# Batch 1's attention moved earlier inside the head of a fused linear-attention and MLP kernel

## Chip, cores, metric

The kernel runs on one core of a Trainium2 chip. The metric is device time of one execution in microseconds (us), median of several runs. Executions of one kernel agree within about 0.3%. All profiles are of core 0. A profile's span is 1.8 to 1.9 us shorter than the timed value, so times are compared with times and spans with spans.

## The reference, cut to what matters

```python
# 8 batches, 8 heads, 576 rows, head size 64
kv  = einsum('bhsd,bhse->bhde', k, v)            # K^T V of each head
out = einsum('bhsd,bhde->bhse', q, kv)           # "scores" below
rms = sqrt(mean(out * out, axis=-1) + 1e-6)
x   = (out / rms * g_norm)                       # -> 4608 tokens x 512
h   = x @ w_in                                   # product one, 512 -> 2048
g   = where(h > 0, h, exp(min(h, 0)) - 1)        # elu
y   = g @ w_out                                  # product two, 2048 -> 512
```

## The kernel before

TensorE works through nine groups of 512 tokens: batches 0 to 7 (512 of the 576 rows of each) and a ninth group of the remaining rows. While it computes one batch's two products, the next batch's attention is slipped in between. The work lies in the head of the kernel, where batch 0's product two runs and batch 1's attention is made for the first time.

The kernel fills eight banks of PSUM, TensorE's output memory (a bank is here the room of 512 fp32 values in each partition): one tile `at` of two banks, two tiles of two banks in the pool `ps_m1`, two tiles of one bank in `ps_m2`. A tile is the unit in which the program reserves this memory. Batch 0's output has four token tiles j of 128 tokens. Tiles 2 and 3 are the two halves of one `ps_m1` tile; tiles 0 and 1 have a `ps_m2` tile each.

```python
def mm2(T, j, f0, f1, hold=False):
    if f0 == 0 and (T, j) not in o_ps:
        o_ps[T, j] = ps_m2.tile([P, DM], FP32, name="o_ps", tag="mm2")
    for f in range(f0, f1):
        nc.tensor.matmul(o_ps[T, j], lhsT=gT[T][:, f, j * P : j * P + P],
                         rhs=w_out_sb[:, f, :], start=(f == 0), stop=(f == FC - 1))
    if f1 == FC and not hold:
        mm2_out(T, j)                   # ScalarE copies o_ps to o_sb; a store after odd j

# x_t(h): turn one half of the scaled rows (xs) and copy it out with g_norm
def turn(ps=None):
    if h == 0:
        st["xt"] = at_tile(BF16).rearrange("p (h c t) -> p h c t", h=2, c=KC)
    xt = st["xt"][:, h]                 # x0 and x1: two halves of the same PSUM tile ...
    if ps is not None:
        xt = ps.bitcast(BF16)...        # ... unless another one is given
    # 8 transposes into xt; then x0 is copied by ScalarE, x1 by VectorE

# ---- loads (cut) ----
edges = (0, 512, 1024, 1536, 2048)      # w_in in four pieces
...
for name in "kv": fetch_packed_kv(name, 1, slice(0, 2))   # first halves of K and V
load_w_out(8, 10)
for name in "kv": fetch_packed_kv(name, 1, slice(2, 4))   # second halves

# ---- batch 0's product two with batch 1's attention inside (cut) ----
both = ps_m1.tile([P, 2, G], FP32, name="o_ps", tag="mm1")
for a in range(2):
    o_ps[0, 2 + a] = both[:, a, :]
order = (2, 3, 0, 1)
for j in order: mm2_quarter(0, j, 0)
at["q"]()                               # q transposes
for j in order: mm2_quarter(0, j, 1)
mm2(0, order[0], 8, 10)
at["kv"]()                              # K^T V
for j in order[1:]: mm2(0, j, 8, 10)
at["se"]({0: None, 1: ps_m1.tile(...)}) # scores; then squares, sums, inverse roots, xs
...
for j in order: mm2(0, j, 10, 12)
for j in order:
    mm2(0, j, 12, FC, hold=j in (2, 3))
    if j == 3:
        mm2_out(0, 2)
        mm2_out(0, 3)
    if j == 0:
        at["x0"]()
...
# ---- batch 1's product one: first two tiles in column halves (cut) ----
for cs in (slice(0, 256), slice(256, G)):
    for f in range(4):
        ...                             # 4 matmuls, 128x256
        if cs.start == 0 and f == 1:
            head_x1()                   # x1 of batch 1
...
# ---- one batch later (cut) ----
at["x0"]()
mm2_quarter(1, 2, 0)
at["x1"](ps_m1.tile([P, 2, G], FP32, name="xt_ps", tag="mm1")[:, 0, :])
mm2_quarter(1, 2, 1)
```

`hold` delays the copies of output tiles 2 and 3 until tile 3 is done.

Of the kernel before, what the change touches and what calls it, by code (L numbers as in the profile page):

```python
# [8 lines left out]
FP32 = mybir.dt.float32  # L9
BF16 = mybir.dt.bfloat16  # L10
# [6 lines left out]
def kernel(  # L17
# [13 lines left out]
    nc = tc.nc  # L31
    P = 128
# [6 lines left out]
    G = J * P  # L39
    RK = S // 64  # L40
    KC = DM // P
    FC = DF // P
# [7 lines left out]
    mlpg = ctx.enter_context(tc.tile_pool(name="mlpg", bufs=2))  # L50
# [13 lines left out]
    w_in_sb = const.tile([P, KC, DF], BF16, name="w_in_sb")  # L64
# [49 lines left out]
    def fetch_packed_kv(name, b, hs=slice(0, 4)):  # L114
        in_ = (k if name == "k" else v)[b].rearrange("h r d -> (h r d)").rearrange(
            "(h p x) -> p h x", h=4, p=P
        )
        nc.gpsimd.dma_start(  # L118
            out=raw[name, b].rearrange("p h j d -> p h (j d)")[:, hs], in_=in_[:, hs]
        )  # L120
# [19 lines left out]
    def load_w_out(f0, f1):  # L140
        fs = slice(f0, f1)
        nc.gpsimd.dma_start(
            out=w_out_sb[:, fs, :], in_=moe_w_out.rearrange("(c p) f -> p c f", p=P)[:, fs, :]
        )
# [17 lines left out]
    xT = {}  # L162

    def at_tile(dtype):
        full = ps_at.tile([P, 1024], FP32, name="at", tag="at")
        return full if dtype == FP32 else full.bitcast(BF16)
# [210 lines left out]
    gT = {}  # L377

    def mm1(T, i, cols=(slice(0, 512),), relu=False, home="m1", between=()):

        if i == 0:
            gT[T] = mlpg.tile([P, FC, G], BF16, name="gT", tag="gT")
        x = xT[T]
        if home == "m2":
            h_ps = [ps_m2.tile([P, G], FP32, name="h_ps", tag="mm2") for _ in range(2)]
            parts = [(a, a + 1, h_ps[a].rearrange("p (a t) -> p a t", a=1)) for a in range(2)]
        else:
            if home == "at":
                both = at_tile(FP32).rearrange("p (a t) -> p a t", a=2)
            else:  # L390
                both = ps_m1.tile([P, 2, G], FP32, name="h_ps", tag="mm1")
            h_ps = [both[:, a, :] for a in range(2)]
            parts = [(0, 2, both)]
        for cs in cols:
            for a in range(2):
                f = 2 * i + a
                for c in range(KC):
                    nc.tensor.matmul(  # L398
                        h_ps[a][:, cs],
                        lhsT=w_in_sb[:, c, f * P : f * P + P],  # L400
                        rhs=x(c, cs),
                        start=(c == 0),
                        stop=(c == KC - 1),
                    )
        return elu(T, i, parts, relu, between)

    def elu(T, i, parts, relu, between=()):
        e = mlpt.tile([P, 2, G], BF16, name="elu_e", tag="elu_e")
        for lo, hi, ps in parts:
            nc.scalar.activation(e[:, lo:hi, :], ps, AF.Exp)  # L410
        for piece in between:
            piece()
        if relu:
            h = mlpt.tile([P, 2, G], BF16, name="elu_h", tag="elu_h", bufs=2)
            for lo, hi, ps in parts:
                nc.scalar.activation(h[:, lo:hi, :], ps, AF.Relu)  # L416
            parts = [(0, 2, h)]

        def rest():
            for lo, hi, h in parts:  # L420
                nc.vector.tensor_scalar(  # L421
                    out=e[:, lo:hi, :],
                    in0=e[:, lo:hi, :],
                    scalar1=1.0,
                    scalar2=1.0,
                    op0=ALU.min,
                    op1=ALU.subtract,
                )
                nc.vector.tensor_tensor(  # L429
                    out=gT[T][:, 2 * i + lo : 2 * i + hi, :],  # L430
                    in0=e[:, lo:hi, :],
                    in1=h,
                    op=ALU.add if relu else ALU.max,
                )

        return rest
# [3 lines left out]
# [5 lines that stand above are left out]
            nc.tensor.matmul(  # L445
                o_ps[T, j],
                lhsT=gT[T][:, f, j * P : j * P + P],
                rhs=w_out_sb[:, f, :],
                start=(f == 0),
                stop=(f == FC - 1),  # L450
            )
        if f1 == FC and not hold:
            mm2_out(T, j)

    def mm2_out(T, j):
        if j % 2 == 0:
            o_sb[T] = outp.tile([P, 2, DM], FP32, name="o_sb", tag="o")
        nc.scalar.copy(o_sb[T][:, j % 2, :], o_ps.pop((T, j)))  # L458
        if j % 2 == 1:
            store(T, j // 2)  # L460

    def mm2_quarter(T, j, i):
        mm2(T, j, 4 * i, 4 * i + 4)

    def store(T, half):
        if T < B:
            nc.sync.dma_start(
                out=out[T * S : T * S + G, :].rearrange("(p j) f -> p j f", j=J)[
                    :, 2 * half : 2 * half + 2, :
                ],  # L470
                in_=o_sb[T],
            )
        else:
            rows = out.rearrange("(i l s) f -> l s i f", l=2, s=S)
            for l in range(2):
                nc.sync.dma_start(
                    out=rows[l, G:S, 2 * half : 2 * half + 2, :],
                    in_=o_sb[T][l * 64 : l * 64 + 64, :, :],
                )
# [7 lines left out]
    for c in range(4):  # L487
# [1 line left out]
        if c == 2:  # L489
            make_identity(nc, ident)  # L490
        fetch_packed_kv("v", 0, slice(c, c + 1))
    edges = (0, 512, 1024, 1536, 2048)
    for lo, hi in zip(edges, edges[1:]):
        load_w_in(slice(lo, hi))
    load_w_out(0, 4)
# [2 lines left out]
    packed_kv(1)  # L498
    for name in "kv":
        fetch_packed_kv(name, 1, slice(0, 2))  # L500
    load_w_out(8, 10)
    for name in "kv":
        fetch_packed_kv(name, 1, slice(2, 4))

    zeros = const.tile([P, 512], BF16, name="zeros")
    nc.vector.memset(zeros, 0.0)  # L506
# [55 lines left out]
    x0 = attp.tile([P, KC, G], BF16, name="xT", tag="xT")  # L562
# [41 lines left out]
    def first(fs, cs):  # L604
# [33 lines left out]
        lhsT=g_row.rearrange("p l d -> p (l d)"),  # L638
        rhs=one,
        start=True,  # L640
        stop=True,
# [48 lines left out]
    ps_m1 = ctx.enter_context(tc.tile_pool(name="ps_m1", bufs=2, space=bass.MemoryType.PSUM, reuse_waits="tile"))  # L690
    ps_m2 = ctx.enter_context(tc.tile_pool(name="ps_m2", bufs=2, space=bass.MemoryType.PSUM, reuse_waits="tile"))

    at, ahead = attention(1), attention(2)
# [14 lines left out]
    order = (2, 3, 0, 1)  # L708
    for j in order:
        mm2_quarter(0, j, 0)  # L710
    at["q"]()
    for j in order:
        mm2_quarter(0, j, 1)
    mm2(0, order[0], 8, 10)
    at["kv"]()
    for j in order[1:]:
        mm2(0, j, 8, 10)
    at["se"]({0: None, 1: ps_m1.tile([P, 2, G], FP32, name="se_ps", tag="mm1")})
    for n in range(2):
        at[f"sq{n}"]()  # L720
# [2 lines left out]
        at[f"inv{n}"]()  # L723
    at["mul0"]()
    at["mul1"]()
    for j in order:
        mm2(0, j, 10, 12)
    unpack_q(2, Q)
    ahead["qd"]()
    for j in order:  # L730
        mm2(0, j, 12, FC, hold=j in (2, 3))
        if j == 3:
            mm2_out(0, 2)
            mm2_out(0, 3)
        if j == 0:
            at["x0"]()

    def fetch(b):
        if b < B:
# [51 lines left out]

    ahead["landed"]()
    fetch(3)
    head_x1 = at["x1"]
    at, ahead = ahead, attention(3)
    ahead["qd"]()
    gT[1] = mlpg.tile([P, FC, G], BF16, name="gT", tag="gT")
    firsts = [ps_m1.tile([P, 2, G], FP32, name="h_ps", tag="mm1") for _ in range(2)]
    for cs in (slice(0, 256), slice(256, G)):
        for f in range(4):  # L800
            for c in range(KC):
                nc.tensor.matmul(  # L802
                    firsts[f // 2][:, f % 2, cs],
                    lhsT=w_in_sb[:, c, f * P : f * P + P],
                    rhs=xT[1](c, cs),
                    start=(c == 0),
                    stop=(c == KC - 1),
                )
            if cs.start == 0 and f == 1:
                head_x1()  # L810
    for i in range(8):
        if i < 2:
            elu(1, i, [(0, 2, firsts[i])], i == 0)()
        else:
            mm1(1, i, relu=i == 4, home="m2" if i in (2, 5) else "m1")()
        if i == 3:
            at["kv"]()
    mm2(1, 0, 0, 8)
# [16 lines left out]
    for T in range(2, NT):  # L835
        at = ahead if T + 1 < NT else None
# [17 lines left out]
    for j, cols in pieces:  # L854
        n = cols.stop - cols.start
        ps = ps_m2.tile([P, DM], FP32, name="o_ps", tag="mm2")[:, 0:n]
        for f in range(FC):
            nc.tensor.matmul(  # L858
                ps,
                lhsT=gT[B][:, f, j * P : j * P + P],  # L860
                rhs=w_out_sb[:, f, cols],
                start=(f == 0),
                stop=(f == FC - 1),
# [35 lines left out]
```

## Time and profile before

| | before |
|---|---|
| time, median of 6 runs | 285.50 us |
| TensorE busy | 97% of the span, full clock |
| start of product two of batch 0 | 29.07 us |
| start of batch 2's K^T V, after four tiles of batch 1's product one | 54.37 us |

Lines of the page of the kernel before: the span, the busy times of the engines with their instruction counts, the granted clock in 40 slices, and the shares of the chain that ended last.

```profile
span 283.7 us, 5180 instructions
...
PE 274.4 (97%) x2131; PEld 130.5 (46%) x2162; DVE 159.9 (56%) x231; ACT 153.1 (54%) x220; POOL 53.5 (19%) x94
...
PEclk9999999999999999999999999999999999999999
...
PE 90%; ACT 3%; DVE 3%; DMA 2%; issue 1%; SPq 0%
```

TensorE bounds the kernel; only its idle moments can be won. They are found in the timeline of TensorE alone, kernel before. The columns are start, duration, engine, line, operation, out<-in, tile and count; what is in brackets is the idle time before the group and what ended it. PE is TensorE, ACT ScalarE, DVE VectorE. Lines L445 and L398 are the matmuls of products two and one, L802 the column-half block. `at<-v_pk,k_pk` is K^T V, `<-kv_sb,qT` the scores, `<-ident,xs` the x transposes.

```profile
29.07 3.62 PE L445 MATMUL o_ps<-w_out_sb,gT 128*128 128x512 bf16 x15
...
39.73 0.41 PE L201 MATMUL at<-kv_sb,qT 64*128 64x64 bf16 x16
...
40.30 4.49 PE L445 MATMUL o_ps<-w_out_sb,gT 128*128 128x512 bf16 x19
44.83 0.62 PE L305 MATMUL at<-ident,xs 128*128 128x128 bf16 x8
45.29 1.03 PE L445 MATMUL o_ps<-w_out_sb,gT 128*128 128x512 bf16 x4
46.69 1.03 PE L802 MATMUL h_ps<-xT,w_in_sb 128*128 128x256 bf16 x8 [0.37 <-ACT xT L312]
47.55 0.61 PE L305 MATMUL at<-ident,xs 128*128 128x128 bf16 x8
48.00 2.99 PE L802 MATMUL h_ps<-xT,w_in_sb 128*128 128x256 bf16 x24
51.04 3.40 PE L398 MATMUL h_ps<-xT,w_in_sb 128*128 128x512 bf16 x15
54.37 0.78 PE L174 MATMUL at<-v_pk,k_pk 64*64 64x64 bf16 x72
...
70.89 0.61 PE L305 MATMUL xt_ps<-ident,xs 128*128 128x128 bf16 x8
71.34 1.03 PE L445 MATMUL o_ps<-w_out_sb,gT 128*128 128x512 bf16 x4
72.35 1.90 PE L398 MATMUL h_ps<-xT,w_in_sb 128*128 128x512 bf16 x7
```

Full-width matmuls (128x512) start every 215.8 ns, the mean of the 948 starts without a break in this trace. A printed idle time is not all that is lost: the end of a matmul is modelled and lies about 0.16 us after the moment at which the next could have started. So the rule is to take the last start, add 0.216, and compare with the next start. The four matmuls at 45.29 should have been followed at 46.15; product one came at 46.69, so 0.53 us were lost, and the wait is for ScalarE's copy of x0 (`ACT xT`). Another 0.2 us were lost ahead of 44.83 (waiting for xs) and, in the single records inside the group at 48.00, 0.2 ahead of the second column half (waiting for x1).

Waits of TensorE from 29 to 52 us, kernel before (total us, times, longest); only the longest entry is shown:

```profile
PE h_ps L802 <- ACT xT L312: 0.4, 1, 0.4
```

ScalarE in the same place, kernel before:

```profile
44.08 1.54 ACT L458 COPY o_sb<-o_ps 128x512 f32<-128x512 f32 x3
45.49 1.14 ACT L312 ACTIVATE xT<-at,g_col 128x1024 bf16<-128x1024 bf16 x1
```

The three output copies (tiles 2, 3 and 0) run back to back after the last inverse root; x0's copy follows.

### The profile page before, as it was taken

How to read it: one execution, taken by the hardware profiler on the slowest of the kernel's cores; microseconds unless marked ns; L12 is line 12 of the kernel's file. 1: busy time of each engine (PE TensorE's matmuls, PEld its weight loads, DVE VectorE, ACT ScalarE, POOL GpSimd, SP SyncE). 2: the span in 40 equal slices, each digit the busy share in tenths (PEclk: the TensorE clock that was granted, in tenths of full speed). 3: DMA queues.
4: the chain of work that ended last, by engine and by line, in shares of the span. 5: the costliest groups of instructions: out<-in, count | busy, mean ns of one | idle time of the engine just before them, and what ended most of it. 6: DMA issues, size and time to landing. Idle time of an engine off the chain costs nothing.

```text
span 283.7 us, 5180 instructions
## 1 busy us (share of the span) xinstructions
PE 274.4 (97%) x2131; PEld 130.5 (46%) x2162; DVE 159.9 (56%) x231; ACT 153.1 (54%) x220; POOL 53.5 (19%) x94
## 2 busy tenths in 40 slices
PE   6999999999999999999999999999999999999994
PEld 2444555545544444445444444444444444444443
DVE  2359315698478636934695468544864486444400
ACT  2779535766496338634773378246923692333311
POOL 7823402251421060104210421012000000000000
PEclk9999999999999999999999999999999999999999
DMA  7999999796993598356944794355253123010122
GB/s 194 204 207 202 207 201 178 225 143 113 196 190 68 150 134 181 76 148 90 208 95 127 105 213 94 98 130 148 49 93 83 77 48 100 2 74 0 74 75 75
DMA packets 55979, 35.99 MB, mean 127 GB/s; under 512 B 32788, under 2 KB 53524, under 8 KB 55956
## 3 DMA queue, kind: packets, MB, share of 16 engines
q0 software_dynamic: 20208, 17.30, 39.7%
q1 hardware_dynamic: 35348, 17.83, 23.6%
q10 hardware_dynamic: 400, 0.52, 0.5%
q8 instruction: 17, 0.28, 0.4%
q14 instruction: 6, 0.05, 0.0%
HBM read 36.70 MB, written 9.44 MB: 163 GB/s over the span
## 4 chain that ended last, share of the span: by engine, by line
PE 90%; ACT 3%; DVE 3%; DMA 2%; issue 1%; SPq 0%
PE h_ps L398 39%; PE o_ps L445 36%; PE o_ps L858 5%; DMA st_q<-in_q_dram 2%; PE at L174 2%; PE h_ps L802 1%; DVE ss L218 1%; PE at L201 1%; PE bank L607 1%; ACT sq L213 1%; PE at L398 1%; PE bank L577 1%; PE bank L529 1%; ACT o_sb L458 1%; PE se_ps L201 1%
## 5 line engine op out<-in xcount | busy, mean ns | idle before, releaser
L398 PE MATMUL h_ps<-xT,w_in_sb 128*128 128x512 bf16 x524 | 123.6, 380 | 0.2
L445 PE MATMUL o_ps<-w_out_sb,gT 128*128 128x512 bf16 x488 | 117.9, 379 | 1.4 <-issue 0.3
L410 ACT ACTIVATE elu_e<-h_ps 128x1024 bf16<-128x1024 f32 (+1 forms) x72 | 70.8, 991 | 83.8 <-PE h_ps L398 79.2
L398 PEld LDWEIGHTS <-w_in_sb 128*128 128x128 bf16 x536 | 50.8, 98 | 61.5 <-DVE xT L333 1.7
L445 PEld LDWEIGHTS <-gT 128*128 128x128 bf16 x512 | 49.6, 98 | 59.1
L421 DVE TENSOR_SCALAR elu_e<-elu_e 128x1024 bf16<-128x1024 bf16 (+1 forms) x75 | 32.3, 431 | 70.5 <-ACT elu_e L410 70.5
L429 DVE TENSOR_TENSOR gT<-elu_e,h_ps 128x1024 bf16<-128x1024 bf16 (+1 forms) x53 | 62.6, 1181 | 5.9 <-DVE elu_e L421 0.5
L218 DVE TENSOR_REDUCE ss<-sq 128x16 f32<-128x1024 bf16 x16 | 19.3, 1218 | 13.4 <-ACT sq L213 12.7
L458 ACT COPY o_sb<-o_ps 128x512 f32<-128x512 f32 x32 | 18.5, 585 | 14.4 <-PE o_ps L445 14.4
L150 POOL COPY q_bf<-q_pk 128x512 bf16<-128x512 bf16 x24 | 14.6, 636 | 23.5 <-DMA q_pk<-in_q_dram 23.5
L416 ACT ACTIVATE elu_h<-h_ps 128x1024 bf16<-128x1024 f32 (+1 forms) x19 | 18.3, 968 | 0.0
L429 DVE TENSOR_TENSOR gT<-elu_e,elu_h 128x1024 bf16<-128x1024 bf16 x19 | 13.2, 693 | 2.9 <-ACT elu_h L416 1.7
L858 PE MATMUL o_ps<-w_out_sb,gT 128*128 128x512 bf16 (+1 forms) x79 | 14.0, 336 | 0.1
L125 POOL COPY gate<-qT 1x1 bf16<-1x1 bf16 x6 | 1.1, 179 | 59.9 <-DMA qT<-q_bf 59.9
L229 DVE TENSOR_TENSOR xs<-at,ss 128x512 bf16<-128x512 f32 x18 | 11.5, 682 | 1.2 <-ACT ss L225 1.2
L104 POOL DMA_DIRECT2D q_pk<-in_q_dram x14 | 10.5, 759 | 4.7 <-issue 1.9
L213 ACT ACTIVATE sq<-at 128x1024 bf16<-128x1024 f32 x9 | 9.4, 1044 | 2.4 <-PE at L201 2.4
L858 PEld LDWEIGHTS <-gT 128*128 128x128 bf16 x80 | 7.7, 98 | 6.4 <-DVE gT L429 0.4
L118 POOL DMA_DIRECT2D v_pk<-in_v_dram x12 | 8.4, 702 | 5.0 <-DMA w_in_sb<-in_moe_w_in_dram 2.9
L118 POOL DMA_DIRECT2D k_pk<-in_k_dram x12 | 8.3, 694 | 5.1 <-DMA w_in_sb<-in_moe_w_in_dram 3.4
L866 ACT COPY o_last<-o_ps 128x512 f32<-128x512 f32 (+1 forms) x5 | 2.5, 500 | 10.8 <-PE o_ps L858 10.8
L529 PE MATMUL bank<-zeros 128*128 128x512 bf16 x19 | 6.6, 465 | 1.4 <-DVE zeros L506 1.2
(73 smaller groups left out, 138.6 us busy)
## 6 DMA issues: line engine op xcount, KB each, us to landing
out_dram<-o_sb SPq DMA_DIRECT2D x16, 512.0 KB, 3.0
q_pk<-in_q_dram POOLq DMA_DIRECT2D x14, 256.0 KB, 5.0
k_pk<-in_k_dram POOLq DMA_DIRECT2D x6, 576.0 KB, 8.1
v_pk<-in_v_dram POOLq DMA_DIRECT2D x6, 576.0 KB, 12.2
w_in_sb<-in_moe_w_in_dram POOLq DMA_DIRECT2D x4, 512.0 KB, 10.9
w_out_sb<-in_moe_w_out_dram POOLq DMA_DIRECT2D x3, 512.0 KB, 15.5
st_q<-in_q_dram SPq DMA_DIRECT2D x2, 512.0 KB, 4.7
st_q<-in_q_dram SPq DMA_DIRECT2D x16, 64.0 KB, 2.5
```

The source lines that it names most:

```text
L118: nc.gpsimd.dma_start(out=raw[name, b].rearrange("p h j d -> p h (j d)")[:, hs], in_=in_[:, hs])
L150: eng.tensor_copy(out=out_, in_=in_)
L213: nc.scalar.activation(sq, se_ps, AF.Square)
L218: nc.vector.reduce_sum(out=ss, in_=sq.rearrange("p c (h e) -> p (c h) e", h=H), axis=AX.X)
L398: nc.tensor.matmul(h_ps[a][:, cs], lhsT=w_in_sb[:, c, f * P : f * P + P], rhs=x(c, cs), start=(c == 0), stop=(c == KC - 1),)
L410: nc.scalar.activation(e[:, lo:hi, :], ps, AF.Exp)
L416: nc.scalar.activation(h[:, lo:hi, :], ps, AF.Relu)
L421: nc.vector.tensor_scalar(out=e[:, lo:hi, :], in0=e[:, lo:hi, :], scalar1=1.0, scalar2=1.0, op0=ALU.min, op1=ALU.subtract,)
L429: nc.vector.tensor_tensor(out=gT[T][:, 2 * i + lo : 2 * i + hi, :], in0=e[:, lo:hi, :], in1=h, op=ALU.add if relu else ALU.max,)
L445: nc.tensor.matmul(o_ps[T, j], lhsT=gT[T][:, f, j * P : j * P + P], rhs=w_out_sb[:, f, :], start=(f == 0), stop=(f == FC - 1),)
L458: nc.scalar.copy(o_sb[T][:, j % 2, :], o_ps.pop((T, j)))
L858: nc.tensor.matmul(ps, lhsT=gT[B][:, f, j * P : j * P + P], rhs=w_out_sb[:, f, cols], start=(f == 0), stop=(f == FC - 1),)
```

## The change

Its intent: let batch 1's scores start earlier, so that the chain behind them is done in time and x0 and x1 can both be turned and copied inside product two; then product one can start full width without a wait. For that, K and V must land earlier, so w_out rows 8 to 10 go behind them.

```diff
-    edges = (0, 512, 1024, 1536, 2048)
+    edges = (0, 512, 768, 1280, 1664, 2048)
...
     for name in "kv":
         fetch_packed_kv(name, 1, slice(0, 2))
-    load_w_out(8, 10)
     for name in "kv":
         fetch_packed_kv(name, 1, slice(2, 4))
+    load_w_out(8, 10)
...
     for j in order:
         mm2_quarter(0, j, 0)
-    at["q"]()
-    for j in order:
+        if j == order[2]:
+            at["q"]()
+    for n, j in enumerate(order):
         mm2_quarter(0, j, 1)
-    mm2(0, order[0], 8, 10)
-    at["kv"]()
-    for j in order[1:]:
-        mm2(0, j, 8, 10)
+        if n in (1, 2):
+            at[f"kv{n - 1}"]()
     at["se"](...)
...
-    for j in order:
-        mm2(0, j, 10, 12)
+    for f in (8, 10):
+        for j in order:
+            mm2(0, j, f, f + 2)
...
     for j in order:
-        mm2(0, j, 12, FC, hold=j in (2, 3))
-        if j == 3:
-            mm2_out(0, 2)
-            mm2_out(0, 3)
-        if j == 0:
-            at["x0"]()
+        mm2(0, j, 12, FC)
+        if j in (3, 0):
+            at["x0" if j == 3 else "x1"]()
...                                    # the column-half block of batch 1 is removed:
     for i in range(8):
-        if i < 2:
-            elu(1, i, [(0, 2, firsts[i])], i == 0)()
-        else:
-            mm1(1, i, relu=i == 4, home="m2" if i in (2, 5) else "m1")()
+        mm1(1, i, relu=i in (0, 4), home="m2" if i in (2, 5) else "m1")()
```

More of the change, by code (lines that the diff above doesn't have):

```diff
@@ L793 @@
     fetch(3)
-    head_x1 = at["x1"]
     at, ahead = ahead, attention(3)
     ahead["qd"]()
-    gT[1] = mlpg.tile([P, FC, G], BF16, name="gT", tag="gT")
-    firsts = [ps_m1.tile([P, 2, G], FP32, name="h_ps", tag="mm1") for _ in range(2)]
-    for cs in (slice(0, 256), slice(256, G)):
-        for f in range(4):
-            for c in range(KC):
-                nc.tensor.matmul(
-                    firsts[f // 2][:, f % 2, cs],
-                    lhsT=w_in_sb[:, c, f * P : f * P + P],
-                    rhs=xT[1](c, cs),
-                    start=(c == 0),
-                    stop=(c == KC - 1),
-                )
-            if cs.start == 0 and f == 1:
-                head_x1()
     for i in range(8):
-        if i < 2:
-            elu(1, i, [(0, 2, firsts[i])], i == 0)()
-        else:
-            mm1(1, i, relu=i == 4, home="m2" if i in (2, 5) else "m1")()
+        mm1(1, i, relu=i in (0, 4), home="m2" if i in (2, 5) else "m1")()
         if i == 3:
```

## The prediction

> **What bounds the kernel.** TensorE. The page gives PE 274.4 us busy of a 283.7 us span (97%), the granted clock is full throughout, and the chain of waits is 90% PE. VectorE (56%), ScalarE (54%) and DMA have slack except at a few joints. Full-width matmuls (128x512) start every 215.6 ns; the Trainium skill ("TensorE: Matmul & The Clock Gate", the section on 56 ns) states 215.7 ns when warm, so the trace agrees and dense stretches have nothing left. Only bubbles can be won.
>
> **Where the change acts.** Product two of batch 0 starts at 29.07 us (timeline); the third tile of batch 1's product one (the first without split columns) starts at about 50.83 us: 21.76 us. The work inside, costed from this trace: 64 matmuls 13.80; 32 q transposes with switches 1.11; K^T V 0.81; scores 0.67; two x transposes 0.46 each; 16 full-width (or 32 half-width at 108 ns, the same) matmuls 3.45. Sum 20.8 us. So about 1.0 us is lost in bubbles, which the timeline shows: x0's transposes wait about 0.2 us for the scaled rows (xs, DVE ends 44.77); product one then waits 0.53 us for ScalarE's x0 copy (46.15 to 46.69); its second column half waits 0.2 us for DVE's x1 copy.
>
> **What the change does.** No arithmetic is removed. Scores start about 1.65 us earlier (39.73 to about 38.1), since eight rows-8-to-10 matmuls now follow them. Squares to xs took 5.05 us for half 0 and 6.24 us for half 1 after the scores' start; that gives xs at about 43.1 and 44.3. x0 is needed at about 43.8 and x1 at about 45.2: both waits close. x0's copy (1.14 us) hides under two quarters. x1's DVE copy hides under the last quarter except about 0.15 us: the same order already runs one batch later (x1 at 70.89, four matmuls, product one at 72.35) and leaves 0.15 us. Splitting K^T V adds about 0.09 us of switching. Sum after: about 21.0 us, so 0.7 to 0.8 us less on PE, all on the critical path, as PE is dense afterwards.
>
> **Loads.** The software queue's landings follow issue order in this trace, about 1.45 us for 288 KB and 1.25 us for 256 KB (the Trainium skill, "DMA: Bandwidth & Descriptors", queues and rings: each ring is consumed in order). V's second half landed at 37.75, 1.23 us of which was w_out rows 8-10 ahead of it; now about 36.5. PE reaches the second K^T V half at about 36.75: margin 0.2 us only. Rows 8-10 land at about 37.75, needed at 38.65: fine. The new w_in edges make five loads of four; 512-byte rows (q) moved as fast as 1 KB rows here (1.29 against 1.25 us per 256 KB), so little changes; every w_in piece should still land before use (PE waits for none after the first). The extra issue costs GpSimd 0.75 us where it has slack.
>
> **Prediction.** 284.8 us, range 284.2 to 285.4. Faster by over 2%: 1%. Within 2%: 98%. Slower by over 2%: 1%.
>
> **What would show it.** Scores near 38.1 us; no ScalarE wait of product one before batch 1's first tile, one DVE wait of about 0.15 us; third tile of batch 1 at about 50.1; the stretch after that shifted by the same 0.7 us to the end; no PE wait on V or w_out loads. Wrong if V's half lands after 36.75 (PE waits, gain shrinks by as much), if fewer bytes per w_in row slow the queue, if a bubble reappears later (batch 2's q transpose and loads are paced by DMA and do not move), or if the earlier ScalarE copies of product two's results delay x0.

## The result, and the profile after

The changed kernel took 286.28 us (median of 6 runs, 286.22 to 286.41) against 285.50 before (285.43 to 286.08). The ratio is 1.0023 with a 95% interval of 1.001 to 1.0036. Ratios here are the mean time of one kernel's fast runs over that of the other's of the same rounds, so they are not quite the ratios of the medians. The change is a small loss, clear of noise, where 0.7 us of gain was predicted. (It lies within 2%, which the prediction held 98% likely.)

The same lines of the page, kernel after:

```profile
span 284.6 us, 5152 instructions
...
PE 275.4 (97%) x2115; PEld 129.5 (46%) x2146; DVE 160.1 (56%) x231; ACT 153.8 (54%) x221; POOL 54.0 (19%) x95
```

Sixteen matmuls fewer (the half-width ones joined), and yet a longer span. The timeline of TensorE, kernel after:

```profile
29.05 2.75 PE L445 MATMUL o_ps<-w_out_sb,gT 128*128 128x512 bf16 x11
...
36.82 0.48 PE L174 MATMUL at<-v_pk,k_pk 64*64 64x64 bf16 x36
...
38.20 0.41 PE L201 MATMUL at<-kv_sb,qT 64*128 64x64 bf16 x16
...
38.77 4.49 PE L445 MATMUL o_ps<-w_out_sb,gT 128*128 128x512 bf16 x19
43.94 1.02 PE L445 MATMUL o_ps<-w_out_sb,gT 128*128 128x512 bf16 x4 [0.67 <-ACT o_sb L458]
44.80 0.61 PE L305 MATMUL at<-ident,xs 128*128 128x128 bf16 x8
45.24 1.03 PE L445 MATMUL o_ps<-w_out_sb,gT 128*128 128x512 bf16 x4
46.65 0.61 PE L305 MATMUL at<-ident,xs 128*128 128x128 bf16 x8 [0.38 <-ACT xT L312]
47.09 1.03 PE L445 MATMUL o_ps<-w_out_sb,gT 128*128 128x512 bf16 x4
48.17 7.07 PE L398 MATMUL h_ps<-xT,w_in_sb 128*128 128x512 bf16 x31
55.16 0.78 PE L174 MATMUL at<-v_pk,k_pk 64*64 64x64 bf16 x72
```

Up to the scores all is as predicted: K^T V's second half at 36.82 without a wait, scores at 38.20 instead of 39.73. Then two new idle places appear. After 38.77 come 20 matmuls (one record is missing), the last of which starts at 42.88, so the next was due at 43.10; it came at 43.94, 0.84 us late. That is tile 3's last quarter. And x1's transposes at 46.65 were due at 46.11 (the matmul before them starts at 45.89), 0.54 us late. Both waits are for ScalarE, as the waits of TensorE from 29 to 52 us show, kernel after (a third entry, 0.2 us of `issue`, is left out):

```profile
PE o_ps L445 <- ACT o_sb L458: 0.7, 1, 0.7
PE at L305 <- ACT xT L312: 0.4, 1, 0.4
```

ScalarE, kernel after (start, duration):

```profile
43.30 0.58 ACT L458 COPY o_sb<-o_ps 128x512 f32<-128x512 f32 x1 [0.66 <-PE o_ps L445]
...
45.48 1.12 ACT L312 ACTIVATE xT<-at,g_col 128x1024 bf16<-128x1024 bf16 x1
```

The copy of output tile 2 runs from 43.30 to 43.88, and tile 3's first matmul starts 0.05 us after its end. x0's copy runs from 45.48 to 46.60, and x1's first transpose starts 0.05 us after its end. The Trainium skill ("Perfetto Trace Analysis", Identifying Dependency Chains) advises to look at the semaphores that an instruction waits on: in the trace both of these matmuls carry a wait on ScalarE's semaphore, and in the kernel before neither place has a matmul that starts on the heels of such a copy. In both pairs the copy reads one half of a PSUM tile and the matmul writes the other half. No value passes from one to the other.

Product one then starts at 48.17; batch 2's K^T V, the marker used below, at 55.16 against 54.37. From there on the two traces run in step but for 0.1 us at batch 3's first tile.

### The profile page after: what moved, and what is told of

It reads as the page before. It is cut to its first block, busy times and chain, and to the rows that moved or that the text cites. A ratio compares the mean times of both kernels' runs of the same rounds, so it can differ in the third digit from the quotient of the medians.

```text
span 284.6 us, 5152 instructions
## 1 busy us (share of the span) xinstructions
PE 275.4 (97%) x2115; PEld 129.5 (46%) x2146; DVE 160.1 (56%) x231; ACT 153.8 (54%) x221; POOL 54.0 (19%) x95
## 4 chain that ended last, share of the span: by engine, by line
PE 89%; DVE 4%; DMA 2%; ACT 2%; issue 1%; SPq 0%; DVEq 0%
PE h_ps L398 39%; PE o_ps L445 36%; PE o_ps L837 5%; DMA st_q<-in_q_dram 2%; PE at L174 2%; DVE gT L429 1%; PE at L201 1%; DVE xs L229 1%; PE bank L607 1%; DVE ss L218 1%; PE at L398 1%; PE se_ps L201 1%; PE bank L577 1%; PE bank L529 1%; DVE elu_e L421 0%
## 5 line engine op out<-in xcount | busy, mean ns | idle before, releaser
L398 PE MATMUL h_ps<-xT,w_in_sb 128*128 128x512 bf16 x540 | 127.2, 379 | 0.4
L398 PEld LDWEIGHTS <-w_in_sb 128*128 128x128 bf16 x552 | 52.4, 98 | 64.0 <-DVE xT L333 1.7
L529 PE MATMUL bank<-zeros 128*128 128x512 bf16 x19 | 7.4, 511 | 1.4 <-DVE zeros L506 1.2
```

Source lines behind the costliest of these rows:

```text
L398: nc.tensor.matmul(h_ps[a][:, cs], lhsT=w_in_sb[:, c, f * P : f * P + P], rhs=x(c, cs), start=(c == 0), stop=(c == KC - 1),)
```

## The experiments

Theory A: a matmul waits while ScalarE reads the other half of the same PSUM tile; dropping the hold and putting x1 back into x0's tile made two such waits. Theory B: the new load order and the smaller w_in pieces cost the time. Theory C: starting batch 1 full width costs it. All kernels gave correct results. Each was timed in five rounds; the kernel before was timed beside them in every group (medians 285.52, 285.47, 285.58). The changed kernel was timed only for the result above, so differences to it, and between groups, carry about 0.1 us of doubt from that alone; where a step is smaller, the trace decides. The column "stretch" in the table at the end is from the start of product two to the start of batch 2's K^T V, from the traces.

### e1_hold: the hold alone put back

```diff
-        mm2(0, j, 12, FC)
+        mm2(0, j, 12, FC, hold=j in (2, 3))
+        if j == 3:
+            mm2_out(0, 2)
+            mm2_out(0, 3)
```

> The changed kernel with one thing put back: the copies of output tiles 2 and 3 of batch 0 come after the last matmul of tile 3, as before. Theory A (a matmul waits for ScalarE's copy of the other half of the same PSUM tile): tile 3's last quarter starts at about 43.1 instead of 43.94 us, that wait is gone; but the two copies now stand ahead of x0's copy on ScalarE, so x0's copy ends at about 46.35 and x1's transposes (same PSUM tile as x0's) still wait for it: only about 0.25 us gained on the changed kernel, 286.0 us. Theory B (the new load order and edges cost the time): no change, 286.3. Theory C (the full-width first tiles of batch 1 cost it): no change.

Measured: 286.06 us (286.00 to 286.28), ratio 1.0015. TensorE's timeline, e1_hold:

```profile
38.76 5.36 PE L445 MATMUL o_ps<-w_out_sb,gT 128*128 128x512 bf16 x24
...
46.29 0.61 PE L305 MATMUL at<-ident,xs 128*128 128x128 bf16 x8 [0.87 <-ACT xT L312]
```

and ScalarE's:

```profile
44.16 1.07 ACT L458 COPY o_sb<-o_ps 128x512 f32<-128x512 f32 x2 [1.52 <-PE o_ps L445]
45.11 1.13 ACT L312 ACTIVATE xT<-at,g_col 128x1024 bf16<-128x1024 bf16 x1
```

The 24 matmuls from 38.76 now run without a break: tile 3's wait is gone. x0's transposes come 0.85 us earlier (43.95), but x0's copy stands behind the two held copies and starts only 0.37 us earlier (45.11 for 45.48). So x1 now waits 0.87 us for it where it waited 0.38. Only 0.22 us of the 0.84 come back, as expected.

### e2_own_tile: a PSUM tile of its own for x1

```diff
-        if j in (3, 0):
-            at["x0" if j == 3 else "x1"]()
+        if j == 3:
+            at["x0"]()
+        if j == 0:
+            at["x1"](ps_m1.tile([P, 2, G], FP32, name="xt_ps", tag="mm1")[:, 0, :])
```

> The changed kernel with x1's transposes written to a PSUM tile of their own instead of the second half of x0's. Theory A: x1's transposes start at about 46.15 instead of 46.65 us without a wait for ScalarE, product one of batch 1 at about 47.67 instead of 48.17; tile 3's wait of 0.67 us stays: about 285.8 us, 0.5 below the changed kernel. Theories B and C: no change, 286.3.

Measured: 285.59 us (285.43 to 285.73), ratio 0.9996. TensorE's timeline, e2_own_tile:

```profile
43.98 1.02 PE L445 MATMUL o_ps<-w_out_sb,gT 128*128 128x512 bf16 x4 [0.67 <-ACT o_sb L458]
...
46.15 0.61 PE L305 MATMUL xt_ps<-ident,xs 128*128 128x128 bf16 x8
```

and ScalarE's copy of x0 in the same run:

```profile
45.52 1.12 ACT L312 ACTIVATE xT<-at,g_col 128x1024 bf16<-128x1024 bf16 x1
```

x1's transposes start at 46.15, while ScalarE is still reading x0 (45.52 to 46.64). So it was not ScalarE's reading as such that stopped TensorE here, but a read of the same tile. Tile 3's wait stays, as it should. The time fell by 0.69 us, more than the expected 0.5. In the profiles the stretch gave 0.58, and 0.2 came after the last store had landed (see below the table of all runs).

### e3_both: both

```diff
-        mm2(0, j, 12, FC)
-        if j in (3, 0):
-            at["x0" if j == 3 else "x1"]()
+        mm2(0, j, 12, FC, hold=j in (2, 3))
+        if j == 3:
+            mm2_out(0, 2)
+            mm2_out(0, 3)
+            at["x0"]()
+        if j == 0:
+            at["x1"](ps_m1.tile([P, 2, G], FP32, name="xt_ps", tag="mm1")[:, 0, :])
```

> Both put right together. Theory A: neither wait is left, product one of batch 1 starts at about 46.9 us (changed kernel 48.17), its third tile at about 50.3 (before 50.83): about 285.0 us, 0.5 below before and 1.3 below the changed kernel. More than the sum of the two alone (0.25 + 0.5), because each wait hides part of the other. Theories B and C: 286.3.

Measured: 284.77 us (284.58 to 284.86), ratio 0.9967, interval 0.9954 to 0.9979. TensorE's timeline, e3_both:

```profile
38.91 5.35 PE L445 MATMUL o_ps<-w_out_sb,gT 128*128 128x512 bf16 x24
44.10 0.61 PE L305 MATMUL at<-ident,xs 128*128 128x128 bf16 x8
44.55 1.03 PE L445 MATMUL o_ps<-w_out_sb,gT 128*128 128x512 bf16 x4
45.41 0.61 PE L305 MATMUL xt_ps<-ident,xs 128*128 128x128 bf16 x8
45.86 1.03 PE L445 MATMUL o_ps<-w_out_sb,gT 128*128 128x512 bf16 x4
46.87 7.08 PE L398 MATMUL h_ps<-xT,w_in_sb 128*128 128x512 bf16 x32
```

No bracket is left between 38.91 and 46.87. The two repairs alone gave 0.22 and 0.69 us, together 1.51. In the stretch they gave 0.34, 0.58 and 1.42, about the sum of the two waits (0.84 + 0.54). The hold alone falls short because it makes x1's wait longer (e1); with x1 in its own tile it gives the full 0.84. About 0.2 us of the gains of e2 and e3 by the clock came after the last store, as said, and is not the work of these waits. Theories B and C fall: loads and full-width start are those of the changed kernel, and this one beats both kernels. (Of theory C a small part survives, see e6.)

### e4_loads_only: the kernel before with the new loads

```diff
-edges = (0, 512, 1024, 1536, 2048)
+edges = (0, 512, 768, 1280, 1664, 2048)
...
-load_w_out(8, 10)
 for name in "kv":
     fetch_packed_kv(name, 1, slice(2, 4))
+load_w_out(8, 10)
```

> The kernel before with only the load part of the change: five w_in pieces, and w_out rows 8-10 behind the second halves of K and V. Theory A: 285.5 us, within 0.15 of before; rows 8-10 land at about 37.9 us, needed at about 37.1 by the first two matmuls of rows 8-10 in that order, so up to 0.8 us of wait at that place may appear, partly taken back by the later wait for the scaled rows. Theory B: about 286.3 us with a wait for a w_in, K, V or w_out load that the changed kernel shows too.

Measured: 286.59 us (286.46 to 286.70), ratio 1.0031. TensorE's timeline, e4_loads_only:

```profile
38.06 0.59 PE L445 MATMUL o_ps<-w_out_sb,gT 128*128 128x512 bf16 x2 [0.67 <-DMA w_out_sb<-in_moe_w_out_dram]
```

Theory A's 285.5 was missed by 1.1 us. The wait that its expectation named (up to 0.8 us) came in full, and nothing of it was taken back: the stretch is 0.83 us longer than before. By time alone this could pass for theory B (286.3 expected), but the wait is another one: the old order of work asks for rows 8-10 ahead of K^T V, and now they land last. The changed kernel asks for them later and has no such wait. A load order and an order of work belong together.

### e5_before_no_hold: the reverse of e1

```diff
-        mm2(0, j, 12, FC, hold=j in (2, 3))
-        if j == 3:
-            mm2_out(0, 2)
-            mm2_out(0, 3)
+        mm2(0, j, 12, FC)
```

> The kernel before with one thing taken away: output tile 2 of batch 0 is copied out as soon as it is done, not after tile 3. Theory A (sharing a PSUM tile with a tile that ScalarE is reading): tile 3's last quarter waits for that copy, which stands behind the second inverse root on ScalarE (ends 44.17), so it starts at about 44.8 instead of 42.9 us; product one of batch 1 at about 48.4 instead of 46.69; about 1.7 us slower than before, 287.2. Rival: the hold is without effect, 285.5.

Measured: 287.25 us (287.12 to 287.75), ratio 1.0066. TensorE's timeline, e5_before_no_hold, the group that begins with tile 3's last quarter:

```profile
44.62 1.89 PE L445 MATMUL o_ps<-w_out_sb,gT 128*128 128x512 bf16 x7 [1.63 <-ACT o_sb L458]
```

The hold was worth 1.8 us in the kernel before: tile 2's copy stands behind the inverse roots in ScalarE's queue (it runs from 44.00 to 44.57), and tile 3 waits for it.

### e6_both_cols: e3 with the first tile of batch 1 in two column halves

```diff
-        mm1(1, i, relu=i in (0, 4), home=...)()
+        cols = (slice(0, 256), slice(256, G)) if i == 0 else (slice(0, G),)
+        mm1(1, i, cols, relu=i in (0, 4), home=...)()
```

> The kernel of run e3_both, with the first tile of batch 1's product one again in two column halves, the first of which needs x0 alone. Takes away the last wait of the stretch, about 0.2 us for VectorE's x1 copy (46.67 to 46.87 in that run): about 284.6 us. If that wait costs nothing, 284.8.

Measured: 284.48 us (284.44 to 285.09), ratio 0.9968. TensorE's timeline, e6_both_cols:

```profile
45.69 1.03 PE L445 MATMUL o_ps<-w_out_sb,gT 128*128 128x512 bf16 x4
46.55 7.09 PE L398 MATMUL h_ps<-xT,w_in_sb 128*128 128x256 bf16 x39
```

The wait before product one is gone (46.55 is 45.69 and four matmuls), and the stretch fell from 24.69 to 24.55 us. The clock alone would not show it: the ratios to the kernel before are 0.9967 (e3) and 0.9968. The column halves that the change removed had a use: they let product one begin before x1 is copied.

### e7_old_loads: e6 with the loads of the kernel before

```diff
+edges = (0, 512, 1024, 1536, 2048)
-edges = (0, 512, 768, 1280, 1664, 2048)
...
+load_w_out(8, 10)
 for name in "kv":
     fetch_packed_kv(name, 1, slice(2, 4))
-load_w_out(8, 10)
```

> The kernel of run e6_both_cols with the loads as before (four w_in pieces, w_out rows 8-10 ahead of the second halves of K and V). V's second half then lands at about 37.75 us and the second K^T V half, due at about 36.9, waits about 0.85 us for it: about 285.4 us. If the load order did not matter to the new order of work, 284.6.

Measured: 285.75 us (285.64 to 286.11), ratio 1.0007. TensorE's timeline, e7_old_loads:

```profile
38.33 0.48 PE L174 MATMUL at<-v_pk,k_pk 64*64 64x64 bf16 x36 [1.14 <-DMA v_pk<-in_v_dram]
```

The new order of work needs the new order of loads: without it V's second half lands at 38.19 us and TensorE waits for it. The cost, 1.27 us against e6, is more than the 0.85 expected. Part of that was a slip in the expectation: in e6 the half is due at 36.79, not 36.9, and TensorE starts 0.14 us after the landing, so that with the landing of the kernel before the wait is 37.75 + 0.14 - 36.79 = 1.1 us. The profiled run was the slowest of the five, with all its loads some 0.3 us late.

### e8_old_edges: e6 with w_in in four pieces

```diff
-    edges = (0, 512, 768, 1280, 1664, 2048)
+    edges = (0, 512, 1024, 1536, 2048)
```

> The kernel of run e6_both_cols with w_in again in four equal pieces, the new order of K, V and w_out kept. If the five pieces are worth nothing: 284.5 us, within 0.15 of run e6_both_cols, V's second half lands within 0.2 us of there (36.5). If the smaller pieces cost the queue time: V's half lands earlier by that much and the time falls; if they save a wait in the head of the kernel, product two starts later than 29.05 us and the time rises.

Measured: 284.46 us (284.38 to 284.82), ratio 0.9962. Product two starts at 29.01 (e6: 29.02), V's second half lands at 36.44 (e6: 36.52). The five pieces are worth nothing and cost nothing.

### e9_cols_twice: e6 with the same split in batch 2's first tile

```diff
-                rest = mm1(T, i, relu=i in relu, between=early)
+                cols = (slice(0, 256), slice(256, G)) if i == 0 else (slice(0, G),)
+                rest = mm1(T, i, cols, relu=i in relu, between=early)
```

> The kernel of run e6_both_cols, and the same column split in the first tile of batch 2's product one, where the trace shows product one waiting about 0.15 us for VectorE's x1 copy (71.72 to 71.86 in run e3_both): about 284.45 us. If batch 3's first tile, which waits for VectorE as well, takes it back: 284.6.

Measured: 284.38 us (284.24 to 284.82), ratio 0.9962, interval 0.9949 to 0.9974. The trace shows the 0.14 us at batch 2's first tile gone (between the K^T V of batch 2 and of batch 3 19.67 us instead of 19.81). The medians differ by 0.10 us, and the ranges overlap, so that this step helps is shown by the trace rather than by the clock. It has the lowest median of all versions, by 0.08 us from e8, which is within the noise.

### e10_order: the waits hidden by order

```diff
-    for j in order:
+    for j in (2, 0, 3, 1):
         mm2(0, j, 12, FC)
-        if j in (3, 0):
-            at["x0" if j == 3 else "x1"]()
+        if j in (0, 3):
+            at["x0" if j == 0 else "x1"]()
```

(`o_sb` gets a second key so that tiles 2 and 0 do not share a buffer.)

> The changed kernel with nothing put back but the order of the last quarter: tiles 2, 0, 3, 1 in place of 2, 3, 0, 1, x0 after tile 0, x1 after tile 3. Tile 0 has a PSUM tile of its own, so theory A says that it runs while ScalarE copies tile 2, and tile 3's wait is hidden without a hold; x1's transposes still wait for x0's copy (due at about 45.26, start at about 45.9), product one at about 47.4 instead of 48.17: about 285.5 us. If ScalarE's copy holds up TensorE as such, whatever the tile, tile 0 waits as tile 3 did and the time stays at 286.3.

Measured: 285.65 us (285.39 to 285.94), ratio 0.9999. TensorE's timeline, e10_order:

```profile
37.23 0.48 PE L174 MATMUL at<-v_pk,k_pk 64*64 64x64 bf16 x36 [0.50 <-DMA v_pk<-in_v_dram]
...
39.19 5.35 PE L445 MATMUL o_ps<-w_out_sb,gT 128*128 128x512 bf16 x23
44.38 0.61 PE L305 MATMUL at<-ident,xs 128*128 128x128 bf16 x8
```

and ScalarE's copy of output tile 2 in the same run:

```profile
43.71 0.58 ACT L458 COPY o_sb<-o_ps 128x512 f32<-128x512 f32 x1 [0.66 <-PE o_ps L445]
```

Tile 0's last quarter runs right through that copy: the group from 39.19 (24 matmuls, one record missing) has no break. In its single records the four matmuls of tile 0 start at 43.51, 43.73, 43.94 and 44.16, on time, while ScalarE copies from 43.71 to 44.29. The same copy at the same point of the chain stopped tile 3 in the changed kernel. The profiled run was the slowest of the five, and the bracket at 37.23 says why: V's second half came 0.5 us late in it. So the load margin is thin: over the nine profiles with the new load order that half landed between 36.44 and 36.66 us seven times, and at 37.10 and 37.24 in the two others.

### All runs

| run | median us | stretch us |
|---|---|---|
| before | 285.50 | 25.30 |
| changed | 286.28 | 26.11 |
| e1_hold | 286.06 | 25.77 |
| e2_own_tile | 285.59 | 25.53 |
| e3_both | 284.77 | 24.69 |
| e4_loads_only | 286.59 | 26.13 |
| e5_before_no_hold | 287.25 | 26.90 |
| e6_both_cols | 284.48 | 24.55 |
| e7_old_loads | 285.75 | 25.77 |
| e8_old_edges | 284.46 | 24.55 |
| e9_cols_twice | 284.38 | 24.55 |
| e10_order | 285.65 | 25.85 |

The stretch orders the runs nearly as the clock does, and its differences account for most of the time differences. What is left, up to about 0.4 us, is where product two starts (28.90 to 29.34 us in these profiles), the wait at batch 3's first tile (0.1 us), profiles that caught the slowest of the five executions (e7, e10), and the end of the kernel: from the landing of the last store to the end of the span it took 1.2 us in six of the kernels, and 1.0 in e2, e3, e6, e7, e8 and e9. These six are the ones that give x1 its own tile, on all three chips, so the 0.2 us belongs to the program and not to chance. The traces show where it lies: VectorE's last `DRAIN` instruction starts 0.11 us after the semaphore event before it in these six, 0.46 or 0.47 in the others. Why was not tried and stays open.

## Why the prediction was wrong

- "Only bubbles can be won" and the cost of the work in the stretch were right. Repaired, the changed kernel runs product two to the third tile of batch 1 in 46.87 + 16 x 0.2158 - 29.19 = 21.13 us (e3_both); the prediction had "about 21.0". That its time, 284.77, is the predicted 284.8 is partly luck: about 0.2 us of the gain lies at the end of the kernel, which the prediction did not consider.
- "Scores start about 1.65 us earlier" was right (1.53), and so were the times of xs (43.25 and 44.44, for 43.1 and 44.3), the reach of the loads (V's half at 36.66, needed at 36.82) and the harmlessness of the w_in pieces (e8_old_edges). The margin of 0.2 us on V was real: e10_order's profile fell on the wrong side of it.
- The step that failed is "both waits close", with the sum after of "about 21.0 us" in which 64 matmuls of product two run without a break. The changed kernel took 48.17 + 16 x 0.2158 - 29.05 = 22.57 us. The missing terms are 0.84 us at tile 3 and 0.54 us at x1.
- For tile 3, the prediction did not cost the removal of `hold` at all. It asked only whether "the earlier ScalarE copies of product two's results delay x0". They delayed TensorE: e1_hold and e5_before_no_hold show it from both sides, and e10_order shows that the copy stops only the tile that shares its PSUM tile.
- For x1, the failed sentence is "the same order already runs one batch later". It doesn't: there x1 goes into a PSUM tile of its own, and the timeline of before says so (`xt_ps` at 70.89, where the changed kernel has `at` at 46.65). e2_own_tile put that tile in and the wait was gone.
- The wait of "about 0.15 us" for VectorE at product one was there (0.2 us), and e6_both_cols took it away.

What stays open: whether the hardware needs these two waits at all. The Trainium skill ("PSUM — Partial Sum Buffer", PSUM bank collisions raise a hardware error) asks for a guard by bank and quadrant. Half a tile here is 512 fp32 values a partition, which by that page's Specifications is one whole bank, so the two halves lie in different banks, if the tiles start where banks start, and by that page would need no guard. No run here tried it: wherever a matmul was to write one half of a tile while ScalarE's copy of the other half was pending or under way, it waited, so the runs show that sharing a tile brings it, not whether the chip or only the program needs it. Nor did a run give output tiles 2 and 3 a tile each; for tile 3, that the shared tile is the cause rests on e1, e5 and e10 together.

## What to carry to other kernels

When two results share one accumulator tile, the copy that empties one half can stop the engine that fills the other, although no data passes between them: give them separate tiles, hold the first copy until both are filled, or put work on another tile between them. Before removing a flag or an argument that looks idle in the source (`hold`, an extra tile passed to one call), ask what it kept apart; take it away alone and look for the wait. And when two new waits lie on one chain, repair both before judging: here the two repairs gave 0.22 and 0.69 us alone, and 1.51 together (0.2 of the last two at the kernel's end).

## What the Trainium skill lacked or had wrong

- "PSUM — Partial Sum Buffer" gives the bank and quadrant as the unit to guard. It lacks that a program can be built with the whole multi-bank tile as the unit of waiting: 0.84 us (tile 3) and 0.54 us (x1) lost here between halves that, by its bank size, are different banks.
- "DMA: Bandwidth & Descriptors" (Queues, rings and completion order) says of the queues of SyncE and ScalarE that descriptors are consumed in ring order, but that a later one may finish before an earlier one. The loads are in GpSimd's queue, for which it has no measured order of landing: in all twelve profiles every one of the 47 or 48 loads landed in the order of issue. Nor does it give a spread for one load: V's second half landed from 36.44 to 37.24 us over nine profiles with the same order of loads, which is more than the 0.2 us of margin that the schedule had.
- "TensorE: Matmul & The Clock Gate" states 215.7 ns between warm full-width matmuls; the trace has 215.8. Nothing to mend.
- No page tells how a kernel's own end depends on the program: it took 1.2 us from the landing of the last store to the end of the span in six kernels, and 1.0 in the six that give x1 its own tile, and VectorE's last `DRAIN` instruction comes 0.35 us later in the former (0.46 against 0.11 us after its semaphore event).
